# Two buffers for the triangular inversion, row lengths on GpSimd, state sums on TensorE and ScalarE

## The chip, the cores and the metric

The kernel runs on one NeuronCore of a Trainium2 chip. The core has a matrix engine (TensorE, "PE" in the profile, its weight loads "PEld"), a vector engine (VectorE, "DVE"), an activation engine (ScalarE, "ACT"), a general engine (GpSimd, "POOL") and an engine that here only issues transfers (SyncE, "SP"). Each engine takes its instructions strictly in the order of its own queue and waits at the head of that queue for what an instruction needs. Matrix products land in PSUM, which GpSimd can't read in this kernel; everything else lies in SBUF. The metric is the device time of one execution in microseconds (us); lower is better.

## The reference

A gated-delta recurrence over 32 sequences (4 batches of 8 heads, 768 steps, heads of 48), and then a router that sends each of 3072 tokens to two of eight experts:

```python
k_n = k / (np.linalg.norm(k, axis=-1, keepdims=True) + 1e-06)
for t in range(S):
    kt, vt, bt = (k_n[:, :, t], v[:, :, t], beta[:, :, t, None])
    y[:, :, t] = np.einsum('bhd,bhde->bhe', q[:, :, t], state)
    v_old = np.einsum('bhde,bhd->bhe', state, kt)
    state = state + bt[:, :, :, None] * np.einsum('bhd,bhe->bhde', kt, vt - v_old)
...
logits = x @ w_gate
noisy_logits = logits + np.log1p(np.exp(x @ w_noise)) * noise
top2 = np.argpartition(-noisy_logits, 2, axis=1)[:, :2]
...
h = np.maximum(x[mask] @ w1[e], 0.0)
out[mask] += top2_w[mask, k, None] * (h @ w2[e])
```

## The kernel before

**Two stages.** `deltanet` computes the recurrence, the router's choice, and the sending of each token's row to its experts' lists in memory. After it the experts run one after another: products on TensorE that fill it almost wholly. The change touches `deltanet` alone.

**How the recurrence is tiled.** The 768 steps are cut into 12 chunks of 64 (`c`). A unit `n` is one chunk for two of the four batches, so a chunk has two units (`z` 0 and 1). Two chunks, that is four units, make a block `s`; there are six blocks, 0 to 5. Within a chunk the recurrence is a triangular system, which the kernel inverts once for a whole block: 128 triangles of 32 by 32, one on each partition.

**What one block does.**
- `products` (from L509): the keys are transposed on TensorE, multiplied with themselves into a pair of PSUM banks, and ScalarE copies the diagonal squares to `gd` (L546).
- `begin_inversion` and `invert` (L559 to L661), on VectorE: a transposition of `gd` to `t` (L563); the diagonal of `t` is the squared lengths of the keys, copied to `ss` (L581, L582); ScalarE makes the root from logarithm and exponential (L585, L586); eight small VectorE operations make the length `norm`, `d` (beta over length squared) and `minus_d` (L591 to L602); GpSimd meanwhile zeroes all but the lower triangle of `t` (L610); `norm` is transposed to `norms` (L624); `t` is multiplied by `minus_d` (L629); then 30 columns, each a product into `part` (L641) and an addition to `t` (L645); the diagonal is set to one and `t` multiplied by `d` (L657).
- `end_inversion`: two transpositions of `t`, to `tb` (L667) and `tt` (L675).
- `join`: from `tb` and `tt`, TensorE and ScalarE put the 64 by 64 inverses `w64` together (L698 to L736).
- `within`: products of queries and keys, masked by VectorE to `qk` (L760).
- `recur`, once for each unit, the chain of the recurrence: GpSimd scales `v` by the lengths (L779); for `c > 0`, TensorE multiplies the old state by the keys (L517) and VectorE subtracts that from `v` (L798); TensorE solves with `w64` (L808); ScalarE copies the result `u` (L815); TensorE multiplies the keys by `u` into the pair of banks `p_s` (L826); VectorE adds the old state and writes the new one (L838, for the first chunk a copy, L842); GpSimd copies the state in a wider form to `wide` (L851).
- `answer`: the output rows `y`, their transposition and the router's logits.

`route` follows for blocks 0 and 1 together, 2 and 3 together, 4, and 5: some thirty small VectorE operations (L964 to L1041), and then GpSimd's indirect transfers that send the rows (L333, "spread" below; 16 for two blocks, 8 for one). `early` runs five tiles of expert 0 at the end of the stage, on rows that blocks 0 to 4 have sent (loads at L1178, first TensorE work L1206).

**Buffers.** `gd` has two buffers (`two_gds`), `t` has one (`t_inv`), and so have `ss`, `root`, `norm`, `d` and `minus_d`. So the transposition to `t` for a block stands behind `tb` and `tt` of the block before.

**What sets the order.** The pieces are not run as written: `Jobs.order` is a planner that places every piece on its engine with a cost and, for some, a due time, and the program then has each engine's queue in the order that it found. A block's transposition to `t` is due at `FIRST + s * PACE` (13 and 36 us). GpSimd's pieces are also linked in that order.

Of the kernel before, what the change touches and what calls it, by code (L numbers as in the profile page):

```python
# [18 lines left out]
Q = 32  # L19
# [10 lines left out]
INVERSIONS = [(s, 1) for s in range(6)]  # L30
# [152 lines left out]
def kernel(  # L183
# [84 lines left out]

    ones = const.tile([128, 128], FP32, name="ones")
# [110 lines left out]
    def deltanet(ictx):  # L380
# [68 lines left out]
        two_gds = ring([128, UH, Q], "gd", 2)  # L449
        most_steps = max(x for _, x in INVERSIONS)  # L450
        inversion_of = {s + x: g for g, (s, n) in enumerate(INVERSIONS) for x in range(n)}
        t_inv = sb([128, most_steps, Q, Q], "t")
        parts = sb([128, most_steps * 240], "part")
# [69 lines left out]
        def products(n):  # L523
# [14 lines left out]
            gd = two_gds(s).rearrange("p (u j z) i -> p u z j i", u=US, z=2)[:, i]  # L538
            for x, lo in enumerate(range(0, 128, Q)):
                rows, cols = slice(lo, lo + Q), slice(lo % C, lo % C + Q)  # L540
                on, copy = (DVE, nc.vector.tensor_copy) if s == 0 and x % 2 else (
                    ACT, nc.scalar.copy
                )
                jobs.add(
                    on, 0.38,
                    lambda rows=rows, cols=cols, copy=copy: copy(  # L546
                        gd[rows], two_banks(p, C)[rows, :, :, cols]
                    ),
                    writes=[("gd", s % 2, i, lo)], uses=p,
                )  # L550
# [5 lines left out]
        def begin_inversion(s):  # L556

            first_s, steps = INVERSIONS[inversion_of[s]]
            x = s - first_s  # L559
            gd = two_gds(s)  # L560
            jobs.add(
                DVE, 1.95,
                lambda: nc.vector.transpose(  # L563
                    out=t_inv[:, x], in_=gd.rearrange("p h i -> p i h")
                ),
                reads=[("gd", s % 2, i, lo) for i in range(US) for lo in range(0, 128, Q)],
                writes=["t"], due=FIRST + first_s * PACE + 2 * x,
            )

        def invert(g):  # L570

            first_s, steps = INVERSIONS[g]
            t, v_ = t_inv[:, 0:steps], nc.vector
            diagonal = t.rearrange("p s i j -> p s (i j)")[:, :, 0 : Q * Q : Q + 1]
            ss, root, norm, d, minus_d = (x[:, 0:steps] for x in small.values())
            shape = [128, steps, Q, Q]
            soon = FIRST + first_s * PACE + 2 * steps + 1.0
            per = 1.06 * steps

            def squares():  # L580
                v_.tensor_copy(ss, diagonal)  # L581
                v_.tensor_scalar_max(root, ss, 1e-30)  # L582

            def by_log():
                nc.scalar.activation(root, root, ACTF.Ln)  # L585
                nc.scalar.activation(root, root, ACTF.Exp, scale=0.5)  # L586

            def lengths():


                v_.reciprocal(norm, root)  # L591
                v_.tensor_tensor(out=norm, in0=norm, in1=ss, op=ALU.mult)
                v_.tensor_tensor(out=norm, in0=norm, in1=root, op=ALU.add)
                v_.tensor_scalar(
                    out=norm, in0=norm, scalar1=0.5, scalar2=1e-6, op0=ALU.mult, op1=ALU.add
                )
                v_.tensor_tensor(out=d, in0=norm, in1=norm, op=ALU.mult)
                v_.reciprocal(d, d)
                v_.tensor_tensor(
                    out=d, in0=d, in1=beta_b[:, first_s : first_s + steps], op=ALU.mult  # L600
                )
                v_.tensor_scalar_mul(minus_d, d, -1.0)  # L602

            jobs.add(DVE, 0.4, squares, reads=["t"], writes=["ss", "root"], due=soon)
            jobs.add(ACT, 0.5, by_log, writes=["root"], due=soon + 1)

            for x in range(steps):
                jobs.add(
                    POOL, 1.5,
                    lambda x=x: [nc.gpsimd.affine_select(  # L610
                        out=t[:, x], in_=t[:, x], pattern=[[1, Q], [-1, Q]], base=0,
                        channel_multiplier=0, compare_op=ALU.is_gt, fill=0.0,
                    )],
                    reads=["ss"], writes=["t"], due=soon + 3,
                )
            every_beta = [("beta", i) for i in range(128 // H)]
            jobs.add(
                DVE, 2.0, lengths, reads=["root", "ss", *every_beta], writes=["norm", "d"],
                due=soon + 3,
            )  # L620
            for x in range(steps):
                jobs.add(
                    DVE, 0.2,
                    lambda x=x: v_.transpose(out=norms(first_s + x), in_=norm[:, x]),  # L624
                    reads=["norm"], writes=[("norms", (first_s + x) % 3)],
                )
            jobs.add(
                DVE, 0.15 + per,
                lambda: v_.tensor_tensor(  # L629
                    out=t, in0=t, in1=minus_d[:, :, None, :].to_broadcast(shape), op=ALU.mult  # L630
                ),
                reads=["d"], writes=["t"],
# [3 lines left out]
            def column(j):  # L636
                shape = [128, steps, Q - 1 - j, j]
                part = parts[:, 0 : steps * shape[2] * j].rearrange(
                    "p (s i j) -> p s i j", s=steps, j=j
                )  # L640
                v_.tensor_tensor(  # L641
                    out=part, in0=t[:, :, j + 1 :, j, None].to_broadcast(shape),
                    in1=t[:, :, None, j, 0:j].to_broadcast(shape), op=ALU.mult,
                )
                v_.tensor_tensor(  # L645
                    out=t[:, :, j + 1 :, 0:j], in0=t[:, :, j + 1 :, 0:j], in1=part, op=ALU.add
                )

            for j in range(1, Q - 1):
                jobs.add(  # L650
                    DVE, 0.36 + 0.0019 * steps * j * (Q - 1 - j), lambda j=j: column(j),
                    writes=["t", *(("column", first_s + x, j) for x in range(steps))],
                )
            jobs.add(DVE, 0.2, lambda: v_.memset(diagonal, 1.0), writes=["t"])
            jobs.add(
                DVE, 0.15 + per,
                lambda: v_.tensor_tensor(  # L657
                    out=t, in0=t, in1=d[:, :, :, None].to_broadcast(shape), op=ALU.mult
                ),
                reads=["d"], writes=["t"],  # L660
            )  # L661

        def end_inversion(s):
            x = s - INVERSIONS[inversion_of[s]][0]
            jobs.add(
                DVE, 1.95,
                lambda: nc.vector.transpose(  # L667
                    out=tbs.rearrange("p h j -> p j h"),
                    in_=t_inv[:, x].rearrange("p i j -> p j i"),
                ),  # L670
                reads=["t"], writes=["tb"],
# [3 lines left out]
                lambda: nc.vector.transpose(  # L675
                    out=tts.rearrange("p h i -> p i h"), in_=t_inv[:, x]
                ),
                reads=["t"], writes=["tt"],
# [88 lines left out]
        def recur(n):  # L767
# [54 lines left out]
            def gather_state():  # L822
                for j in range(NP):
                    for y in range(2):
                        for b in range(2):
# [3 lines left out]
                                start=(j == 0), stop=(j == NP - 1), skip_group_check=True,  # L829
# [3 lines left out]
                PE, 0.55, gather_state, reads=[u_key, *halves("k", n % NK)], opens=p_s  # L833
            )

            def add_state():
                if c:
                    nc.vector.tensor_tensor(  # L838
                        out=new, in0=two_banks(p_s, D), in1=old, op=ALU.add
                    )  # L840
                else:
                    nc.vector.tensor_copy(new, two_banks(p_s, D))  # L842

            jobs.add(
                DVE, 0.58, add_state, reads=[("st", z, c % N_ST)] if c else [],
# [14 lines left out]
        def answer(n):  # L860
# [71 lines left out]
        small = {  # L932
            x: sb([128, most_steps, Q], x) for x in ("ss", "root", "norm", "d", "minus_d")
        }
# [388 lines left out]
        for s in range(NS):  # L1323
            units = range(s * US, (s + 1) * US)
            g = inversion_of[s]
            if s == INVERSIONS[g][0]:
                for x in range(s, s + INVERSIONS[g][1]):
                    for n in range(x * US, (x + 1) * US):
                        if x:
                            load(n, "k")  # L1330
                        products(n)
                    begin_inversion(x)
                invert(g)
                for x in range(s, s + INVERSIONS[g][1]):
                    for j, cost, moves, emit, writes in large.get(x, ()):
                        jobs.add(
                            SP, cost, emit, writes=writes, lands=2.0, moves=moves,
# [559 lines left out]
```

## Time and profile before

| what | value |
|---|---|
| runs | 870.63, 875.58, 874.54 us; median 874.54 us |
| the profiled execution | 876.77 us, of it 875.0 us span |
| mean granted TensorE clock over the span | 0.905 of full speed |
| busy over the span | TensorE 785.2, VectorE 499.5, ScalarE 309.8, GpSimd 311.4 us |
| start of the transposition to `t`, blocks 0 to 5 | 17.17, 52.01, 98.47, 139.05, 187.78, 230.64 us |
| start of the transposition to `tt`, blocks 0 to 5 | 50.06, 96.09, 136.68, 185.80, 228.62, 287.28 us |
| first TensorE work of `early` | 326.23 us |

The page of a profile gives each engine's busy time, then the span in 40 equal slices with one digit each for the busy share in tenths, and then groups of equal instructions with the number of them, their mean duration, and how long the engine stood idle just before them and who ended that. The table's starts are from the timeline of the trace. About the first 330 us are the recurrence, the rest the experts.

### The profile page before, as it was taken

How to read it: one execution, taken by the hardware profiler on the slowest of the kernel's cores; microseconds unless marked ns; L12 is line 12 of the kernel's file. 1: busy time of each engine (PE TensorE's matmuls, PEld its weight loads, DVE VectorE, ACT ScalarE, POOL GpSimd, SP SyncE). 2: the span in 40 equal slices, each digit the busy share in tenths (PEclk: the TensorE clock that was granted, in tenths of full speed). 3: DMA queues.
4: the chain of work that ended last, by engine and by line, in shares of the span. 5: the costliest groups of instructions: out<-in, count | busy, mean ns of one | idle time of the engine just before them, and what ended most of it. 6: DMA issues, size and time to landing. Idle time of an engine off the chain costs nothing. (4 is left out here: it accounts for less than half of the span.)

```text
span 875.0 us, 21652 instructions
## 1 busy us (share of the span) xinstructions
PE 785.2 (90%) x9166; PEld 602.0 (69%) x9166; DVE 499.5 (57%) x1153; ACT 309.8 (35%) x735; POOL 311.4 (36%) x328
## 2 busy tenths in 40 slices
PE   4758879886899898999999999999999999999995
PEld 3547768685788784566587587587587597597594
DVE  5987798979998632027554454454454454454441
ACT  3573558835743642111420420420420420410510
POOL 3021212021553735025425525525525525515311
PEclk8556759965789798999999999999999999999998
DMA  3789633724433223606324224224225223101201
GB/s 65 134 242 245 137 98 103 196 44 128 130 94 75 105 88 125 244 24 224 102 73 151 92 81 156 78 82 165 66 88 163 60 82 117 57 19 39 56 19 42
DMA packets 119085, 93.77 MB, mean 107 GB/s; under 512 B 84646, under 2 KB 109255, under 8 KB 118976
## 3 DMA queue, kind: packets, MB, share of 16 engines
q1 hardware_dynamic: 107312, 64.54, 26.8%
q0 software_dynamic: 9552, 27.33, 9.2%
q8 instruction: 74, 1.21, 0.6%
q10 hardware_dynamic: 2112, 0.39, 0.3%
q14 instruction: 35, 0.29, 0.1%
HBM read 58.82 MB, written 34.81 MB: 107 GB/s over the span
## 5 line engine op out<-in xcount | busy, mean ns | idle before, releaser
L374 POOL DMA_INDIRECT out_dram<-sums,index x49 | 48.5, 991 | 161.6 <-DVE sums L1386 138.8
L645 DVE TENSOR_TENSOR t<-t,part 128x30 f32<-128x30 f32 (+9 forms) x180 | 66.0, 367 | 6.2
L1498 PE MATMUL a<-xe,w1e 128*128 128x416 f32 x168 | 69.3, 521 | 0.0
L641 DVE TENSOR_TENSOR part<-t 128x30 f32<-128x30 f32 (+9 forms) x180 | 62.1, 345 | 5.0
L365 POOL DMA_INDIRECT sums<-out_dram,index x49 | 50.5, 1031 | 34.1 <-issue 24.0
L851 POOL COPY wide<-st 64x384 f32<-64x384 f32 x44 | 24.6, 559 | 105.3 <-DVE st L838 80.8
L333 POOL DMA_INDIRECT rows_x<-y,slot x48 | 47.1, 981 | 30.3 <-DVE early_gate L353 9.7
L1568 ACT COPY part_c<-c 128x416 f32<-128x416 f32 x28 | 14.2, 506 | 120.9 <-PE c L1498 120.9
L1498 PEld LDWEIGHTS a<-xe,w1e 128*128 128x128 f32 x168 | 29.6, 189 | 31.4 <-issue 17.8
L1559 DVE TENSOR_TENSOR hT<-part,d 128x416 f32<-128x416 f32 x28 | 16.3, 586 | 57.7 <-ACT part L1576 56.2
L1386 DVE SCALAR_TENSOR_TENSOR sums<-d,gate,sums 128x192 f32<-128x192 f32 x56 | 23.3, 416 | 42.5 <-PE d L1498 42.5
L1553 ACT ACTIVATE hT<-hT 128x416 f32<-128x416 f32 x84 | 45.1, 550 | 4.3 <-DVE hT L1559 1.8
L1535 ACT COPY xe<-x 128x384 f32<-128x384 f32 x21 | 10.1, 479 | 100.1 <-PE x L1530 100.1
L808 PE MATMUL single<-v,w 64*64 64x48 f32 x768 | 34.7, 253 | 9.6 <-ACT w L736 3.3
L1498 PE MATMUL d<-xe,w1e 128*128 128x416 f32 x112 | 41.6, 513 | 0.0
L1498 PE MATMUL c<-xe,s_w 128*128 128x416 f32 x112 | 41.4, 512 | 0.0
L1559 DVE TENSOR_TENSOR hT<-part,c 128x416 f32<-128x416 f32 x28 | 16.5, 588 | 41.8 <-ACT part L1587 40.2
L808 PEld LDWEIGHTS single<-v,w 64*64 64x64 f32 x768 | 32.2, 169 | 11.5 <-issue 5.5
L698 ACT COPY w<-tt 32x256 f32<-32x256 f32 x96 | 38.6, 402 | 1.7
L1498 PE MATMUL d<-t_w,hT 128*128 128x192 f32 x224 | 38.6, 326 | 0.0
L610 POOL TENSOR_SCALAR_AFFINE_SELECT t<-t 128x1024 f32<-128x1024 f32 x6 | 7.6, 1272 | 85.7 <-DVE ss L581 52.1
L1459 POOL TENSOR_TENSOR t_w<-w2e,t_w 128x768 f32<-128x768 f32 x14 | 25.4, 1815 | 32.4 <-PE x L1498 32.3
(241 smaller groups left out, 1884.2 us busy)
## 6 DMA issues: line engine op xcount, KB each, us to landing
w1e<-in_moe_w_dram SPq DMA_DIRECT2D x8, 1536.0 KB
w2e<-in_moe_w_dram SPq DMA_DIRECT2D x8, 1536.0 KB
xr<-rows_x SPq DMA_DIRECT2D x7, 1164.0 KB
rows_x<-empty SPq DMA_DIRECT2D x8, 776.0 KB
qp<-in_q_dram SPq DMA_DIRECT2D x48, 96.0 KB
v<-in_v_dram SPq DMA_DIRECT2D x48, 96.0 KB
out_dram<-empty SPq DMA_DIRECT2D x4, 1152.0 KB
kp<-in_k_dram SPq DMA_DIRECT2D x44, 96.0 KB
```

The costliest lines, as they stand in the source:

```text
L333: d = nc.gpsimd.indirect_dma_start(out=rows_x, out_offset=bass.IndirectOffsetOnAxis(ap=slot, axis=0), in_=rows, in_offset=None,).ins
L365: nc.gpsimd.indirect_dma_start(out=got, out_offset=None, in_=out, in_offset=bass.IndirectOffsetOnAxis(ap=index, axis=0), bounds_check=N - ...
L374: nc.gpsimd.indirect_dma_start(out=out, out_offset=bass.IndirectOffsetOnAxis(ap=index, axis=0), in_=got, in_offset=None, bounds_check=N - ...
L641: v_.tensor_tensor(out=part, in0=t[:, :, j + 1 :, j, None].to_broadcast(shape), in1=t[:, :, None, j, 0:j].to_broadcast(shape), op=ALU.mult,)
L645: v_.tensor_tensor(out=t[:, :, j + 1 :, 0:j], in0=t[:, :, j + 1 :, 0:j], in1=part, op=ALU.add)
L698: lambda rows=rows, cols=cols, w64=w64, tt=tt: nc.scalar.copy(w64[rows, :, cols], tt[rows]),
L808: nc.tensor.matmul(per_head(p_u)[b, h], w64[b, h], v_n[b, h], start=(h == 0), stop=(h == H - 1), skip_group_check=True,)
L851: nc.gpsimd.tensor_copy(wide[rows, :, :, y * D : (y + 1) * D], new[rows])
L1459: nc.gpsimd.tensor_tensor(out=out, in0=a, in1=b, op=ALU.subtract)
L1498: nc.tensor.matmul(p, lhsT, rhs, start=opens and i == 0, stop=i == len(products) - 1, skip_group_check=True,)
L1553: relu = lambda m, l, src: nc.scalar.activation(hT[:, m, half[l]], src, ACTF.Relu)
L1559: nc.vector.tensor_tensor(out=hT[:, m, half[l]], in0=x, in1=y, op=ALU.add)
```

## The change

**Inversion.** `gd` gets one buffer and `t` two, and the small tiles come in two sets. The transposition to `t` is due 6 us earlier (`EARLIER`). The lengths are made by one piece of twenty small operations on GpSimd, each on 128 partitions by 32 elements: a copy, six operations with constants and thirteen with two tensors, two of these a power (exponents -0.5 and -1, held in a tile `powers`). The power's root is refined by two Newton steps, the inverse by one. The triangle is cut (affine select) by GpSimd behind that piece in its queue. ScalarE's logarithm and exponential and VectorE's small operations of the inversion are gone.

**States.** For `c > 0` TensorE first multiplies the old state by the identity into the two banks, two products of 128 by 128 by 192, and the products of keys and `u` are added on top; ScalarE copies the sum to the new state. VectorE has no part in it.

**Order.** The planner is given the new costs, so the queues come out in another order. In the built kernel the transposition to `t` for block 1 stands on VectorE's queue behind column 12 of block 0, for block 2 right behind `tt` of block 0, for block 3 behind column 20 of block 2, for block 4 just ahead of `tb` and `tt` of block 3, and for block 5 behind column 24 of block 4.

```diff
-INVERSIONS = [(s, 1) for s in range(6)]
+EARLIER = 6.0
...
+    powers = const.tile([128, 2], FP32, name="powers")
+    for i in range(2):
+        nc.vector.memset(powers[:, i : i + 1], (-0.5, -1.0)[i])
...
-        two_gds = ring([128, UH, Q], "gd", 2)
-        t_inv = sb([128, most_steps, Q, Q], "t")
+        gds = sb([128, UH, Q], "gd")
+        t_invs = ring([128, Q, Q], "t", 2)
...
-            def squares():
-                v_.tensor_copy(ss, diagonal)
-                v_.tensor_scalar_max(root, ss, 1e-30)
-
-            def by_log():
-                nc.scalar.activation(root, root, ACTF.Ln)
-                nc.scalar.activation(root, root, ACTF.Exp, scale=0.5)
-
-            def lengths():
-                v_.reciprocal(norm, root)
-                v_.tensor_tensor(out=norm, in0=norm, in1=ss, op=ALU.mult)
-                v_.tensor_tensor(out=norm, in0=norm, in1=root, op=ALU.add)
-                v_.tensor_scalar(
-                    out=norm, in0=norm, scalar1=0.5, scalar2=1e-6, op0=ALU.mult, op1=ALU.add
-                )
-                v_.tensor_tensor(out=d, in0=norm, in1=norm, op=ALU.mult)
-                v_.reciprocal(d, d)
-                v_.tensor_tensor(
-                    out=d, in0=d, in1=beta_b[:, first_s : first_s + steps], op=ALU.mult
-                )
-                v_.tensor_scalar_mul(minus_d, d, -1.0)
...
+            soon = FIRST + s * PACE - EARLIER
+            def lengths():
...
+                made = [
+                    g.tensor_copy(ss, diagonal),
+                    ts(root, ss, 1e-30, 0.0, ALU.max),
+                    tt(root, root, power(0), ALU.pow),
+                ]
+                for _ in range(2):
+                    made += [
+                        tt(d, ss, root), tt(d, d, root), ts(d, d, -0.5, 1.5), tt(root, root, d),
+                    ]
+                return made + [
+                    tt(norm, ss, root), ts(norm, norm, 1.0, 1e-6),
+                    tt(root, norm, norm), tt(d, root, power(1), ALU.pow),
+                    tt(minus_d, root, d), ts(minus_d, minus_d, -1.0, 2.0), tt(d, d, minus_d),
+                    tt(d, d, beta_b[:, s]), ts(minus_d, d, -1.0, 0.0),
+                ]
...
+            jobs.add(
+                POOL, 3.4, lengths, reads=[*mine("t"), *every_beta],
+                writes=mine("norm", "d"), due=soon + 4,
+            )
+            jobs.add(
+                POOL, 1.5,
+                lambda: [nc.gpsimd.affine_select(
+                    out=t, in_=t, pattern=[[1, Q], [-1, Q]], base=0, channel_multiplier=0,
+                    compare_op=ALU.is_gt, fill=0.0,
+                )],
+                reads=mine("d"), writes=mine("t"), due=soon + 5,
+            )
...
             def gather_state():
+                if c:
+                    for b in range(2):
+                        nc.tensor.matmul(
+                            two_banks(p_s, D)[:, b], ident, old[:, b], start=True, stop=False,
+                            skip_group_check=True,
+                        )
                 for j in range(NP):
...
-                                start=(j == 0), stop=(j == NP - 1), skip_group_check=True,
+                                start=(j == 0 and not c), stop=(j == NP - 1), skip_group_check=True,
...
-            def add_state():
-                if c:
-                    nc.vector.tensor_tensor(
-                        out=new, in0=two_banks(p_s, D), in1=old, op=ALU.add
-                    )
-                else:
-                    nc.vector.tensor_copy(new, two_banks(p_s, D))
-
             jobs.add(
-                DVE, 0.58, add_state, reads=[("st", z, c % N_ST)] if c else [],
+                ACT, 0.5, lambda: nc.scalar.copy(new, two_banks(p_s, D)),
                 writes=[("st", z, (c + 1) % N_ST)], closes=p_s,
             )
```

## The prediction

> **What bounds the kernel now.** First the span in 40 slices (a digit is the busy share of a slice of 21.9 us in tenths):
>
> ```profile
> PE   4758879886899898999999999999999999999995
> DVE  5987798979998632027554454454454454454441
> PEclk8556759965789798999999999999999999999998
> ```
>
> VectorE is at 7 to 9 in the slices behind the first up to the thirteenth (285 us), TensorE at 9 from the seventeenth on, with the clock at 9. So two stages: up to about 290 us VectorE is mostly the fullest, behind it TensorE. What shortens the first moves the second forward and leaves it as long as it is. The windows, cut at the starts of the inversions, say the same with numbers (the columns are window, length, busy us and count for TensorE, weight loads, VectorE, ScalarE, GpSimd, then granted clock, transfer share, GB/s):
>
> ```profile
> 52.00:98.00 46.00, 33.80 (x967) 30.45 (x966) 37.43 (x88) 20.97 (x52) 9.01 (x13) 0.69 0.94 252
> 98.00:139.00 41.00, 33.40 (x873) 29.52 (x872) 34.75 (x87) 27.70 (x73) 6.75 (x9) 0.67 0.40 93
> 139.00:188.00 49.00, 43.50 (x1148) 38.77 (x1146) 43.21 (x116) 32.18 (x84) 8.56 (x13) 0.84 0.56 140
> 188.00:231.00 43.00, 32.64 (x810) 27.79 (x808) 35.96 (x90) 26.07 (x67) 11.27 (x16) 0.62 0.35 96
> 231.00:289.00 58.00, 51.91 (x1566) 47.06 (x1564) 52.59 (x133) 27.27 (x71) 30.77 (x40) 0.94 0.38 102
> 289.00:331.00 42.00, 36.25 (x953) 31.66 (x953) 18.77 (x72) 25.37 (x74) 23.52 (x28) 0.88 0.30 104
> ```
>
> TensorE is not far behind VectorE, at a clock that is often low; the reader should keep that for the rivals. Third, who VectorE waited for from 17 to 290 us, which is nearly all of its idle time that has a name:
>
> ```profile
> DVE norm L591 <- ACT root L586: 14.3, 6, 4.6
> DVE v L798 <- PE pair L517: 4.9, 4, 2.9
> DVE st L842 <- PE pair L826: 1.4, 1, 1.4
> ```
>
> 14.3 us are waits for ScalarE's root, 6.3 us for the recurrence.
>
> **What comes off VectorE.** The ten small operations of an inversion have mean rows of 188 (L581), 194, 353, 397, 286, 274, 420, 352, 191 and 181 ns (L602), together 2.84 us, six times 17.0 us. The wait for the root goes with them, 14.3 us. Of the state sums
>
> ```profile
> L838 DVE TENSOR_TENSOR st<-pair,st 128x384 f32<-128x384 f32 x20 | 10.7, 546 | 0.0
> ```
>
> 18 start before 289 us, 9.8 us, and the two copies of L842 1.1 us. Gross: 17.0 + 14.3 + 10.9 = 42.2 us.
>
> **What is paid for it, by parts.**
>
> *1. The first block has no cover.* Before, 3.4 us lie between the end of the transposition to `t` (19.1 us) and its multiplication (22.5 us), and they are in the gross. Now twenty GpSimd operations and the affine select stand there. No row has these shapes: copies of 128x8 to 128x16 on GpSimd took 0.17 to 0.20 us each where nothing held them, a product of 128x384 took 0.83 us. I take 0.2 us for eighteen. A power has no row; between a plain operation, 0.2 us, and GpSimd's longest elementwise row (t_w, 128x768, 1.8 us) I take 0.4 us, as it has 32 columns. So 18 x 0.2 + 2 x 0.4 = 4.4 us of lengths, with the affine select (1.27 us) and 0.3 us of signals 6.0 us (4.6 to 9.2).
>
> *2. The affine select runs beside columns.* At 235.78 us one stood beside a VectorE operation on two SBUF tensors:
>
> ```profile
> 235.67 1.29 POOL L610 TENSOR_SCALAR_AFFINE_SELECT t<-t 128x1024 f32<-128x1024 f32 x1
> 235.78 1.22 DVE L592 TENSOR_TENSOR norm<-norm,ss 128x32 f32<-128x32 f32 x1
> ```
>
> L592 takes 0.21 us alone, so it lost 1.0 us. Five blocks, one of which paid this before: 4 us (0 to 6.4).
>
> *3. The lengths run beside columns.* Columns are operations on two SBUF tensors too. What GpSimd's product does to one:
>
> ```profile
> 203.16 0.93 DVE L645 TENSOR_TENSOR t<-t,part 128x150 f32<-128x150 f32 x1
> 203.09 0.83 POOL L779 TENSOR_TENSOR v<-v,norms 128x384 f32<-128x384 f32 x1 [1.40 <-DMA v<-in_v_dram]
> ```
>
> L645 of this shape takes 0.32 us alone: 0.61 us lost in a GpSimd operation of 0.83 us. By columns that is 0.05 us for 32, and thirteen such operations with seven cheaper ones make 0.8 us for a block, 4 us for five (2 at the least, 22 if each of the 4.4 us falls on VectorE).
>
> The Trainium skill, in "SBUF — State Buffer", section "SBUF: two separate sides", speaks against the change here: VectorE operations with two SBUF inputs and GpSimd operations share a port pair under an exclusive lock, and the loser blocks for the whole instruction. By that rule all 4.4 us of a block fall on VectorE, 22 us, and the sum below would be 18 us worse, slower than before. The row at 203 us shows a block of three quarters of the instruction, so part of it runs outside of the lock; how much of a small one does, no row shows.
>
> *4. The recurrence of block 0 starts later.* `tt` of block 0 ends 2.6 us later by part 1 (6.0 less 3.4), 2.0 us by block 1's transposition among its columns, and 2 us by parts 2 and 3, so 6.6 us. The multiplication of block 1 comes at 52.0 + 6.6 + 2.0 (block 2's transposition), as before at 59.9. Behind it VectorE reaches the first subtraction from `v` (L798, 77.1 us before, 25 us behind `tt`) and there it already waited, 5 us with L842. It now waits about 5 us more (0 to 8): block 1's own saving is spent there.
>
> *5. Block 4's cover is short.* Between its transposition and its multiplication stand only `tb`, `tt` and some seven short operations, 3.9 + 1.4 us, against 4.4 + 1.3 us and whatever GpSimd loses to the lock: 1.5 us (0 to 5). Blocks 1, 2, 3 and 5 have 10 us and more of columns there.
>
> *6. The tail.* The choice of route for blocks 2 and 3 stood ahead of the last inversion's end: its slots were made at 280.6 us, with `tt` at 287.3 us. In the new queue they stand behind `tt`. So GpSimd's sixteen sends, 1.27 us apart, end some 8 us later against `tt`, and the first loads of `early` (318.9 us, which wait for the last send) with them. Half is covered by TensorE, busy 36.25 of 42 us in that window: 3.5 us (0 to 8). Queued behind these sends are `v` and `wide` of the last chunks; in the new queue four sends stand ahead of `v`, before there were nine, so the recurrence itself loses little.
>
> *7. TensorE.* Forty more products of 128x192, 326 ns each at full clock (row of the experts' L1498 at that shape), 13 us, at half clock up to 26 us. ScalarE gets 22 copies of 128x384 at 0.48 us and loses the logarithms, +8 us; its 46 to 68% use from 52 to 231 us covers that, and without cover it would cost 8 us. From 98 to 289 us TensorE is busy 161.5 of 191 us; after the savings there are about 167 us, and some 9 us are added. It fits only because the clock rises with density: 33 ns for each product at clock 0.94 (231 to 289 us), 40 ns at 0.62 (188 to 231 us). I charge 5 us (0 to 15).
>
> **Sum.** 42.2 - 6.0 - 4 - 4 - 5 - 1.5 - 3.5 - 5 = 13.2 us off the profiled execution's 876.8 us, 863.6 us. That execution lies 2.2 us above the median of the runs, so against the median 861.3 us; I say 862 us. With all parts at their low ends the gain is 36 us, at their high ends the change loses 31 us. Neither will happen in all parts together; from 5 to 28 us of gain, 847 to 870 us, is the likeliest case's own range.
>
> **The rivals.**
>
> *A, TensorE or the recurrence takes VectorE's place.* For it: 161.5 us of work in 191 us, the low clock, the later choice of route in the new queue, which says that the recurrence lags the inversions. Against: TensorE's time shrinks as it is filled. If it does not, and half of the former 29.5 us of idle time stays, the stretch can't be shorter than 161.5 + 9 + 15 = 185.5 us: 5.5 us gained, less the tail's 3.5: 872 us.
>
> *B, slower: GpSimd's small operations block the columns.* Place: the columns beside which the lengths run, in five blocks. Price: at 4.4 us whole, 22 us instead of 4, and the gain of 13 becomes a loss of 5. If the lock also holds GpSimd back behind each column, lengths take 8 us: 3.6 us more in block 0 and 3.6 in block 4. Together about 12 us slower, 887 us. It decides once VectorE loses over (13.2 + 4) / 5 = 3.4 us to the lengths of a block. A power of over 5 us each would do the same by parts 1 and 5. For it: the 1.0 us at 235.78 us. Against: `wide` copies of 0.6 us at 214.8 us cost two columns 0.2 us each.
>
> *C, everything is covered.* The recurrence of block 0 catches up by its shorter path (state sums no longer queue behind columns), the clock goes to full, the tail keeps its length: parts 4, 6 and 7 fall away, 13.5 us more gain: 848 us, and with the locks of part 3 at their low end 846 us.
>
> **How the numbers follow.** Likeliest case 0.56, A 0.17, B 0.18, C 0.09. A measurement here tells from no change what is over 0.5%, 4.4 us. The likeliest case and C are faster, and so are 0.07 of A; 0.10 of A and 0.01 of B lie within; 0.17 are slower. So 0.72, 0.11, 0.17. The range runs from C's 846 us to 880 us, which takes in B's price at 4.4 us of lengths.
>
> **What would show it.** The inversions' starts closer by 5 to 8 us from block 2 on, and hardly at block 1; the wait for L586 gone from VectorE and a wait of about 5 us more for L517 in block 1; twenty GpSimd operations in 4 to 6 us, columns beside them longer by about 1 us a block; TensorE's clock higher between 98 and 270 us; the experts' stage as long as it is. I am wrong if the columns' mean rises from 0.36 us by over 0.05 us (360 of them, 18 us), if VectorE waits for GpSimd in several blocks, or if TensorE is the engine that VectorE waits for.

## The result, and the profile after

| kernel | median | lowest to highest, runs | profiled execution, its span |
|---|---|---|---|
| before | 875.06 us | 870.63 to 879.21, 4 | 876.77, 875.0 us |
| changed | 903.59 us | 898.90 to 905.59, 4 | 905.59, 903.9 us |

The changed kernel takes 1.0319 times as long (95% interval 1.0251 to 1.0388): slower by 28.5 us, where 12.5 us faster was forecast. Experiments 1 to 4 ran on a chip on which the kernel before took 873.97 us, the eight runs of experiments 5 to 9 on two others, on which it took 908.57 and 905.63 us; a kernel is therefore compared by its ratio to the kernel before on the same chip.

The busy shares in 40 slices, now of 22.6 us:

```profile
PE   4446988795895989999999999999999999999995
DVE  4396886974949622204564355355444444354342
PEclk9855779876996969999999999999999999999998
```

VectorE, at 7 to 9 in most of these slices before, now falls to 3 and 4 between the nines: it stands still again and again. The windows, cut near the starts of the transposition to `tt` (window, length, busy us and count for TensorE, weight loads, VectorE, ScalarE, GpSimd, then granted clock, transfer share, GB/s):

```profile
67.00:109.00 42.00, 31.59 (x876) 28.08 (x876) 32.35 (x72) 19.32 (x47) 26.75 (x34) 0.59 1.01 255
109.00:146.00 37.00, 32.87 (x938) 29.05 (x936) 33.03 (x75) 28.56 (x75) 15.28 (x21) 0.86 0.32 73
146.00:198.00 52.00, 42.89 (x1073) 37.64 (x1072) 41.27 (x102) 31.57 (x82) 18.39 (x24) 0.82 0.49 132
198.00:254.00 56.00, 43.69 (x1221) 37.05 (x1220) 39.15 (x84) 31.61 (x79) 42.38 (x51) 0.83 0.48 131
254.00:308.00 54.00, 41.32 (x1085) 36.50 (x1086) 40.17 (x99) 24.13 (x63) 23.50 (x35) 0.84 0.19 43
```

In the last three windows VectorE is busy 120.6 of 162 us, and no other engine is fuller than TensorE's 127.9. So something waits. VectorE's waits from 17 to 320 us name it (us in total, times, longest):

```profile
DVE t L630 <- POOL t L618: 40.2, 4, 14.1
DVE norms L625 <- POOL norm L581: 9.6, 1, 9.6
DVE v L791 <- POOL v L772: 8.7, 2, 7.9
DVE v L791 <- POOL d L578: 6.3, 1, 6.3
```

The 14.3 us of waits for ScalarE's root are gone, and the waits for GpSimd are 64.8 us, where the kernel before had 7.2 us in the same window. L630 is the multiplication by `minus_d` (L629 before), L618 the triangle cut behind the lengths, L625 the transposition of `norm`, L772 the scaling of `v` and L791 the subtraction from it; L578 and L581 are the two helpers that issue the small operations. In GpSimd's timeline of block 0 (start, duration) one sees what takes so long:

```profile
18.82 0.23 POOL L589 COPY ss<-t 128x32 f32<-128x32 f32 x1 [10.68 <-DVE t L606]
...
19.58 5.46 POOL L578 TENSOR_TENSOR root<-root,powers 128x32 f32<-128x32 f32 x1
25.12 0.25 POOL L578 TENSOR_TENSOR d<-ss,root 128x32 f32<-128x32 f32 x1
...
28.68 5.42 POOL L578 TENSOR_TENSOR d<-root,powers 128x32 f32<-128x32 f32 x1
...
35.67 1.27 POOL L618 TENSOR_SCALAR_AFFINE_SELECT t<-t 128x1024 f32<-128x1024 f32 x1
```

Same line, same shape, 5.46 and 0.25 us: the two long ones are the powers. The other eighteen start about 0.33 us apart. The lengths take 16.9 us, and VectorE's multiplication starts at 36.98 us, against 22.53 before (first the line of before, then of the changed kernel):

```profile
22.53 1.22 DVE L629 TENSOR_TENSOR t<-t,minus_d 128x1024 f32<-128x1024 f32 x1
36.98 1.84 DVE L630 TENSOR_TENSOR t<-t,minus_d 128x1024 f32<-128x1024 f32 x1 [8.46 <-POOL t L618]
```

Where the span went is best read as a ledger of three times from the traces: the end of the last transposition to `tt`, the end of the last copy of `u` (the recurrence is done), and the span.

| kernel | last `tt` ends | last `u` ends (behind `tt`) | span (behind `u`) |
|---|---|---|---|
| before | 289.2 | 315.0 (25.8) | 875.0 (560.0) |
| changed | 308.1 | 349.9 (41.8) | 903.9 (554.0) |
| no powers (1) | 274.9 | 312.1 (37.2) | 866.1 (554.0) |
| state part alone (2) | 281.9 | 318.1 (36.2) | 878.2 (560.1) |
| state part taken back (3) | 305.6 | 333.6 (28.0) | 890.9 (557.3) |
| true cost in the plan (4) | 292.1 | 322.8 (30.7) | 881.8 (559.0) |

So of the 28.9 us more of span, 18.9 are lost by the inversions and 16.0 between the last inversion and the end of the recurrence, and 6.0 come back in the experts' stage.

### The profile page after: what moved, and what is told of

Same layout as the page of the kernel before. It is cut to its first block, busy times and chain, and to the rows that moved or that the text cites. A ratio compares the mean times of both kernels' runs of the same rounds, so it can differ in the third digit from the quotient of the medians.

```text
span 903.9 us, 21908 instructions
## 1 busy us (share of the span) xinstructions
PE 793.7 (88%) x9246; PEld 608.5 (67%) x9246; DVE 476.9 (53%) x1073; ACT 315.3 (35%) x745; POOL 408.9 (45%) x448
## 5 line engine op out<-in xcount | busy, mean ns | idle before, releaser
L644 DVE TENSOR_TENSOR t<-t,part 128x30 f32<-128x30 f32 (+9 forms) x180 | 68.7, 382 | 6.2
L640 DVE TENSOR_TENSOR part<-t 128x30 f32<-128x30 f32 (+9 forms) x180 | 66.9, 372 | 5.2
L548 ACT COPY gd<-pair 32x256 f32<-32x256 f32 x88 | 31.9, 362 | 26.6 <-PE pair L519 22.5
L519 PE MATMUL pair<-kT 64*64 64x64 f32 x768 | 22.6, 275 | 20.9 <-DVE qk L753 17.5
L711 PE MATMUL single<-tb,at 32*32 32x32 f32 x768 | 24.4, 219 | 16.6 <-ACT u L808 9.2
```

The costliest lines, as they stand in the source:

```text
L548: lambda rows=rows, cols=cols, copy=copy: copy(gd[rows], two_banks(p, C)[rows, :, :, cols]),
L640: v_.tensor_tensor(out=part, in0=t[:, j + 1 :, j, None].to_broadcast(shape), in1=t[:, None, j, 0:j].to_broadcast(shape), op=ALU.mult,)
L644: v_.tensor_tensor(out=t[:, j + 1 :, 0:j], in0=t[:, j + 1 :, 0:j], in1=part, op=ALU.add)
L711: nc.tensor.matmul(p_x()[dn, h], ats(n)[up, h % 2, h // 2], part_of(tbs, n)[up, h], start=(h == 0), stop=(h == H - 1), skip_group_check=True,)
```

## The experiments

Theory P: the powers. Rivals: S, the state part; C, GpSimd's small operations against VectorE's columns. Unless a number is called a ratio, times are medians.

**1. The powers left out.** Same queues, same number of operations.

```diff
-                    tt(root, root, power(0), ALU.pow),
+                    ts(root, root, -1.6, 2.4),
...
-                    tt(root, norm, norm), tt(d, root, power(1), ALU.pow),
+                    tt(d, root, root), tt(root, norm, norm),
```

> The changed kernel with the two powers of each block left out: the root starts from a straight line in the squared length (one operation with two constants) and the inverse from the square of the root, so the lengths keep twenty small operations in the same order and the queues do not change; the root is only good to some parts in a thousand. Theory P (the powers at 5.45 us each are what went wrong): a block's lengths take about 18 x 0.33 = 6 us in place of 17, block 0's first product (L630) starts near 26 us in place of 36.98, VectorE's wait for the triangle cut (L618, 40.2 us) falls below 10 us, and the time is 855 to 872 us. Theory S (state sums on TensorE and ScalarE, and the later recurrence, are the loss): that wait falls too, but the time stays at 885 us or more. Theory C (small GpSimd operations and VectorE's columns hinder each other): column means stay above 0.372 us and the time is 875 to 890 us.

Measured: 868.31 us against 873.97 (ratio 0.994, 0.9906 to 0.9973). The multiplication of block 0 starts at 26.07 us (first line). VectorE's waits in the same window as above follow, longest first:

```profile
26.07 1.23 DVE L630 TENSOR_TENSOR t<-t,minus_d 128x1024 f32<-128x1024 f32 x1 [2.96 <-POOL t L618]
...
DVE v L791 <- PE pair L519: 10.2, 3, 4.7
DVE v L791 <- POOL v L772: 8.0, 2, 7.2
DVE t L630 <- POOL t L618: 7.4, 3, 3.4
```

The wait for the triangle cut falls from 40.2 to 7.4 us, and the time by 35 us, more than the change had lost. P is shown; S asked for 885 us or more and falls as the main cause. The mean of the columns' additions and products is 391 and 387 ns, above C's mark of 372, but the time is below C's 875 us: the columns do pay, without deciding, and not to the lengths. In the trace of the changed kernel 55 column operations lie wholly within powers, and they took together 0.24 us longer than the quickest of their shapes; the 37 that touch a small operation of the lengths lost 0.53 us. They pay mostly to the scaling of `v`: the 15 columns that it overlaps more than any other GpSimd operation does lost 9.6 us, against 9 columns and 4.1 us before the change, and in this run 20 columns and 11.6 us.

**2. The state part alone**, put into the kernel before: the two products with the identity, ScalarE's copy, VectorE's additions gone.

> The kernel before with the state part alone: the old state goes to the PSUM pair by two products with the identity, ScalarE copies the sum. Theory P: this part is not the loss; VectorE sheds 10.9 us of additions, TensorE takes 40 products of 0.326 us more, and the time is 866 to 877 us against 875 before. Theory S: the longer step of the recurrence (two products and a copy behind it) shows at its full length 20 times, and the time is 882 us or more.

Measured: 880.01 against 873.97 us (1.0062, 1.0034 to 1.009): neither range was met. VectorE does get done earlier, the last `tt` ends 7.3 us sooner, but the recurrence ends 3.1 us later (36.2 us behind `tt` in place of 25.8). VectorE has been relieved of work that did not set the end.

**3. The state part taken back out of the changed kernel**, powers kept: the removed lines of the change's second half put back.

> The changed kernel with the state sums put back on VectorE (additions from PSUM, as before the change); powers and two buffers stay. Theory P: the time stays between 898 and 915 us, since the waits for GpSimd stay. Theory S: it falls to 890 us or less.

Measured: 892.96 us (1.0203, 1.0147 to 1.026), 10.6 us less than the changed kernel, between the two ranges. The waits for GpSimd stay (L618 17.0, L625 9.5, L772 22.3 us), so the powers stay the greater part, and the state part is a second loss: behind the last `tt` the recurrence needs 28.0 us, with the state part 41.8.

The traces show where. Before the change TensorE begins to join the last block (L718, now L711) 1.9 us behind `tt`; in the changed kernel, where `tt` ends at 308.1 us, its queue reads:

```profile
316.57 0.88 PE L865 MATMUL single<-wide,qT 128*64 128x96 f32 x16
319.69 1.94 PE L876 MATMUL single<-u,qk 64*64 64x48 f32 x32 [2.24 <-DVE qk L753]
...
327.04 1.16 PE L711 MATMUL single<-tb,at 32*32 32x32 f32 x34
```

The join stands ready for 18.9 us behind the outputs of block 4. These wait for VectorE's mask L753, that stands behind a subtraction, and the subtraction waits for GpSimd:

```profile
318.48 0.56 DVE L791 TENSOR_TENSOR v<-v,pair 128x384 f32<-128x384 f32 x1 [7.93 <-POOL v L772]
```

GpSimd in turn had stood at `wide` and a send before it came to `v` (three sends stand ahead of these lines):

```profile
315.80 0.50 POOL L843 COPY wide<-st 64x384 f32<-64x384 f32 x1 [2.57 <-DMA rows_x<-y,slot]
316.58 0.98 POOL L337 DMA_INDIRECT rows_x<-y,slot  x1 [0.28 <-POOL wide L843]
317.62 0.82 POOL L772 TENSOR_TENSOR v<-v,norms 128x384 f32<-128x384 f32 x1
```

The join starts behind `tt` by 1.9 us before, 18.9 us changed, 15.3 without powers (1) and 10.7 with the state part alone (2); in experiment 3, with the sums back on VectorE, it starts 3.6 us before `tt` has ended, as soon as `tb` is there. So on this chip the state part is dear in the order that the planner makes of it, at the end. Another order for the join was not tried.

**4. The planner told the truth.** The same instructions.

```diff
-EARLIER = 6.0
+EARLIER = 20.0
...
-                POOL, 3.4, lengths, reads=[*mine("t"), *every_beta],
+                POOL, 17.0, lengths, reads=[*mine("t"), *every_beta],
```

> The changed kernel where only the planner is told otherwise: the lengths cost 17.0 us in place of 3.4, and the transposition to t is due 20 us ahead in place of 6. The instructions are the same, in another order. Theory P with cover to be had: the powers are hidden from block 1 on, VectorE waits for the triangle cut (L618) in block 0 alone (about 14 us), and the time is 865 to 885 us. Theory P without cover (the transposition can't start early enough, or GpSimd's own queue is held up by the lengths): waits of 5 to 15 us stay in three or more blocks, or move to the scaling of v (L772) behind the lengths, and the time is 893 us or more.

Measured: 887.16 us (1.0151, 1.0104 to 1.0198), between the two ranges. The waits for the triangle cut are nearly gone, and a new one stands at the head:

```profile
DVE t L606 <- ACT gd L548: 16.8, 3, 15.1
DVE v L791 <- PE pair L519: 15.4, 4, 5.4
...
DVE t L630 <- POOL t L618: 2.9, 1, 2.9
```

The transposition that was to make the cover is now early for its own input, `gd`. A good half of the loss (903.6 to 887.2 of 28.5 us) came from an order made for lengths of 3.4 us and a transposition 6 us ahead; the two settings were not tried apart. The rest of the powers' price was not hidden so: block 0's multiplication still starts at 36.29 us.

**5. Both undone**: no powers, a third Newton step, and the state sums on VectorE by the edit of experiment 3 (not printed here).

```diff
-                    tt(root, root, power(0), ALU.pow),
+                    ts(root, root, -1.6, 2.4),
...
-                for _ in range(2):
+                for _ in range(3):
...
-                    tt(root, norm, norm), tt(d, root, power(1), ALU.pow),
+                    tt(d, root, root), tt(root, norm, norm),
```

> The changed kernel with both suspected parts undone: no powers (root from a straight line in the squared length, refined by three Newton steps, so 24 small operations and the root good to some parts in a million for these inputs; the inverse from the square of the root), and the state sums back on VectorE. Two losses that add: 868.3 us (no powers) less 6 to 10.6 us (what the state part cost alone, 880.0 - 874.0, and what taking it back gave, 903.6 - 893.0) plus 1 us for the third step: 858 to 864 us, and the stretch from the start of the last transposition to tt to the last copy of u falls from 39 us to about 28 us. If the state part costs only where VectorE has nothing else to wait for: 866 to 872 us.

Measured: 902.62 against 908.57 us (0.9936, 0.9895 to 0.9978). The 858 to 864 us would be ratios of 0.982 to 0.989: not met; the losses did not add. The other case, 866 to 872 us or 0.991 to 0.998, holds. Nor did the last stretch shrink to 28 us: the recurrence ended 36.6 us behind the last `tt`. Part of that belongs to the chip: on it, the kernel before with the seven operations of experiment 8 needs 34.7 us there, against 25.8 in the trace of the kernel before. In the traces from these two chips TensorE stood still for 12 to 18 us between 190 and 345 us ahead of products that waited for nothing that the profile names; in those of both kernels and of experiments 1 to 4 it was 1 to 7 us. Why was not found. It falls into the stretch that the change touches, so a small difference between ratios of different chips proves little. Repeated on the other of the two chips:

> The kernel without powers and with the state sums on VectorE once more. If 0.9936 holds: 0.989 to 0.998, and taking the state part out brings nothing beyond leaving the powers out (0.994). If two losses add: 0.981 to 0.988, as first expected.

Measured: 0.9951 (0.9917 to 0.9986), the same again: without powers this form gains half a per cent with the state part (experiment 1, on another chip) and without it.

**6. Lengths made as before the change** (VectorE and ScalarE), buffers and state part as changed.

> The changed kernel with the lengths made as before the change (ten small VectorE operations, logarithm and exponential on ScalarE); two buffers and the state part stay. If small VectorE operations lengthen the time one for one as the prediction has it (17.0 us over six blocks) and GpSimd's waits of the run without powers (7.4 + 4.5 us) go in return: 868.3 + 17 - 12 = 873 us, from 869 to 880 us. If the recurrence behind the last inversion sets the end and not VectorE: 864 to 869 us.

Measured: 911.86 against 908.57 us (1.0035, 0.9997 to 1.0073). 869 to 880 us would be 0.994 to 1.007, so the first case holds. Against experiment 1 (0.994) the small operations cost 0.0095, some 8 us, when they stand on VectorE. That speaks for GpSimd as their place, without powers; it compares two chips, and the recurrence here ends 51.8 us behind the last `tt`, so it is not shown.

**7. Two buffers alone**, lengths and state sums as before.

> Lengths and state sums as before the change; only two buffers for t, two sets of small tiles, one gd and the transposition 6 us earlier stay. If two buffers hide VectorE's wait for ScalarE's root (14.3 us before the change): 860 to 868 us. If the ordering gives that back (a block's transposition placed among the columns of the block before, ending that block later): 870 to 878 us.

Measured: 0.9944 (0.9905 to 0.9983), half a per cent faster, about 5 of the 14.3 us; the ranges as ratios were 0.984 to 0.993 and 0.995 to 1.004, so it lies between them. Once more, on the other chip:

> Two buffers alone once more (lengths and state sums as before the change), beside the others on one chip. The run before gave 0.9944 (0.9905 to 0.9983). If that holds: 0.990 to 0.998. If the longer times of that chip made it: 0.998 or more.

Measured: 0.9915 (0.9874 to 0.9956), the case that 0.9944 holds. In this trace the columns take 135.5 us against 128.1 before the change, though no length is made on GpSimd here; the new order alone puts 14 columns beside the scaling of `v` (9 before) and three beside the triangle cut (none before).

**8. The power by itself.** Operations on spare tiles, results unused:

```diff
+    for w in (8, 16, 32, 64):
+        nc.gpsimd.tensor_tensor(
+            out=probe_out[:, 0:w], in0=probe[:, 0:w], in1=probe[:, 0:w], op=ALU.pow
+        )
...
+        out=probe_out[0:32, 0:32], in0=probe[0:32, 0:32], in1=probe[0:32, 0:32], op=ALU.pow
...
+        out=probe_out[:, 0:32], in0=probe[:, 0:32], in1=probe[:, 0:32], op=ALU.mult
```

> The kernel before with seven operations on spare tiles added on GpSimd at its start, whose results are not used: powers on 128 partitions by 8, 16, 32 and 64 elements, on 32 partitions by 32, and an addition and a product on 128 by 32. If the power's cost is by the element along the row: 1.4, 2.7, 5.45, 10.9 us, and 5.45 us on 32 partitions, beside 0.25 us for the addition and the product. If it is a fixed cost of calling a power: about 5 us for all five.

The timeline of GpSimd:

```profile
2.60 1.68 POOL L276 TENSOR_TENSOR probe_out<-probe 128x8 f32<-128x8 f32 x1
...
7.41 5.41 POOL L276 TENSOR_TENSOR probe_out<-probe 128x32 f32<-128x32 f32 x1
...
12.93 10.51 POOL L276 TENSOR_TENSOR probe_out<-probe 128x64 f32<-128x64 f32 x1
...
23.56 5.41 POOL L279 TENSOR_TENSOR probe_out<-probe 32x32 f32<-32x32 f32 x1
...
29.43 0.23 POOL L285 TENSOR_TENSOR probe_out<-probe 128x32 f32<-128x32 f32 x1
```

From 32 to 64 elements a row it grows by 5.10 us, 0.16 us for each element of the row, with about 0.4 us beside that (16 elements took 2.92 us); 32 partitions cost as much as 128. A product of the same shape takes 0.23 us. It is a price by the element, as the first case had it.

**9. Mended: the root on ScalarE, the rest on GpSimd.** ScalarE's logarithm and exponential make the inverse root, one Newton step refines it, and the triangle cut no longer stands behind the lengths.

```diff
+            def by_log():
+                nc.scalar.activation(root, root, ACTF.Ln)
+                nc.scalar.activation(root, root, ACTF.Exp, scale=-0.5)
...
+                    tt(d, ss, root), tt(d, d, root), ts(d, d, -0.5, 1.5), tt(root, root, d),
+                    tt(d, root, root), tt(d, d, beta_b[:, s]), ts(minus_d, d, -1.0, 0.0),
+                    tt(norm, ss, root), ts(norm, norm, 1.0, 1e-6),
```

> A mended form of the changed kernel: GpSimd copies the squared lengths, ScalarE makes the inverse root (logarithm, exponential), GpSimd refines it by one Newton step and makes the lengths and factors in nine operations (11 on GpSimd in all, by 0.33 us: 3.7 us), the triangle cut stands ahead of them; state part as in the change. Theory P: as good as the run without powers or better: ratio to before 0.98 to 0.995, block 0's first product (L629 or L630) at 23 to 25 us. If small operations on GpSimd are no good place even without powers, because VectorE still waits for each of them: ratio 0.995 to 1.01.

Measured: 899.45 against 905.63 us (0.9923, 0.9891 to 0.9954); block 0's multiplication at 22.8 us. And with the state sums on VectorE:

> The same with the state sums back on VectorE. If the state part is a loss of its own (it cost 6 us alone): ratio 0.006 or more below that of the run with it, 0.975 to 0.989. If it costs nothing once the powers are gone (the runs without powers gave 0.994 with it and 0.9936 without it, on two chips): within 0.004 of it. If it is a gain once VectorE is the bound again: 0.005 or more above it.

Measured: 895.59 us (0.9842, 0.9781 to 0.9903), 0.008 below the form with the state part, though the two intervals just overlap. This is the lowest ratio of all forms, with its whole interval below 1; that of two buffers alone on the same chip (0.9874 to 0.9956) overlaps it too. The pair also suggests that VectorE is no longer the bound: with the state part the last `tt` ends at 270.8 us and the last `u` 58.6 us later, without it `tt` ends at 295.6 and `u` 33.2 us later, so both finish their recurrence at 329 us. (In the first of them 32 products of keys and `u`, L824, took 10.5 us from 277.25 us on while seven sends went out on GpSimd; its other such groups take 0.7 to 1.1 us. It is one of the stretches without a named wait of experiment 5, and it weakens the comparison.)

## Why the prediction was wrong

It failed at **part 1**, in one term: "A power has no row; between a plain operation, 0.2 us, and GpSimd's longest elementwise row (t_w, 128x768, 1.8 us) I take 0.4 us". Measured: 5.45 us. The upper bound was a row of another operation, and it was taken for a bound because that row was larger, although the power costs 0.16 us for each element of the row (experiment 8). The same part's other eighteen operations cost 0.33 us each by their spacing, not 0.2. Block 0's multiplication therefore came 14.4 us later, where part 1 and its 3.4 us of credit gave 2.6; without the powers it came 3.5 us later.

**Part 5** named the mechanism and the place ("Blocks 1, 2, 3 and 5 have 10 us and more of columns there") and was mis-sized by the same term: a cover of 10 us was enough for 5.7 us of lengths and cut, and not for 18. The multiplications of blocks 3, 4 and 5 waited 6.5, 14.05 and 11.2 us, where 1.5 us was charged for block 4.

**The gross** was right. VectorE's busy time fell by 22.6 us; the small operations (17.0) and the state sums (10.9) make 27.9, less 7.5 us by which the columns grew (128.1 to 135.6 us), which leaves 20.4 us. The wait for the root went too, and another took its place.

**Parts 2 and 3**, 8 us together, gave the right sum: the columns grew by 7.5 us in the changed kernel and by 11.9 us without powers. The rule of the Trainium skill ("SBUF — State Buffer", "SBUF: two separate sides") would, by the estimate made from it, have put 22 us on VectorE for lengths of 4.4 us; in the trace the columns beside the lengths lost 0.24 + 0.53 us in all (experiment 1). The measurement decides: neither powers nor small operations held the columns for long. So the size of parts 2 and 3 was right by luck, and its cause was not. The columns grew beside the scaling of `v`, 9.6 us in place of 4.1, and beside sends and the triangle cut, 1.9 and 0.9 us in place of 0.1 and none. The prediction's own row at 203 us was such a scaling; its price was carried over to the small operations, which barely hold a column, while the new order put more columns beside `v` itself.

**Part 4** foresaw 5 us more of waiting for L517 (now L519). In the changed kernel VectorE waited 3.7 us for it, since other waits came first, and 10.2 us without powers, against 4.9 before. At the place that part 4 named, the first two subtractions, it was 7.0 us without powers against 3.6 before: right in kind once the powers are gone, and somewhat less than 5 us more.

**Part 6**, the tail, was charged 3.5 us (0 to 8). The recurrence ended 16.0 us later behind the last `tt`, without powers 11.4 us. The late choice of route was there, but the sentence "the recurrence itself loses little" is what failed: the join of the last block stood behind outputs of block 4, whose states now come by TensorE and ScalarE. Experiments 2 and 3 tie this to the state part on their chip (experiment 5, on another, found no gain from taking it out), and with it **rival A** came true in part: without powers (0.994, A's 872 us would be 0.997) the recurrence had taken VectorE's place.

**Part 7**: the clock did rise, from 0.76 to 0.85 between 98 and 270 us and to 0.89 without powers, and in the changed kernel VectorE waited little for TensorE (3.7 us).

The sum without the mis-priced term comes near: 862 us forecast, 868.31 measured without powers, 6 us more. In part that is luck. By the ledger the inversions gained 14.3 us, where the sum has 16.7 ahead of the tail; the tail lost 11.4 us, where 3.5 was charged; and 6.0 us that nothing in the sum forecast came back in the experts' stage. **Rival B** had the direction and, in a half sentence ("A power of over 5 us each would do the same by parts 1 and 5"), the cause, but it got its chance from the lock and not from the power. That the high ends of all parts together gave a loss of 31 us, near the 28.5 lost, is chance. The range ended at 880 us because one unpriced operation was spread over small bounds.

## What to carry to other kernels

An operation without a row is not bounded by larger operations of another kind: where the queue of everything else hangs behind it, its price has to be measured first, or the forecast has to carry a case in which it is twenty times a product. Work that is moved to a free engine is free only while its cover is longer than it is; compare the two lengths block by block, the first block above all, and give a planner the true ones. And relieving the fullest engine pays only until the next chain: here the recurrence ended 3 us later and 3 us earlier where the last inversion ended 7 and 14 us earlier.

## What the hardware showed unasked

- A power on GpSimd costs 0.16 us for each element of a row whatever the number of partitions (5.41 us for 32 partitions and for 128), over twenty times a product (0.23 us).
- Small operations of 128 by 32 that follow each other on GpSimd start 0.33 us apart although each takes 0.25 us (block 0 of the changed kernel; 0.39 and 0.41 us apart in blocks 1 and 2).
- A GpSimd product of 128 by 384 (0.83 us) lengthened one column beside it by 0.61 us (at 203.16 us before) and another by 0.69 us (at 218.14 us in the changed kernel), while the 55 columns inside powers of 5.45 us lost 0.24 us together.
- The experts' stage became 6.0 us shorter behind the recurrence (560.0 to 554.0 us) in the changed kernel and without powers, by 2.7 and 1.0 us in experiments 3 and 4, and not with the state part alone. The first 20 us of `early` ran at a granted clock of 1.00 in place of 0.83; by an estimate from these two numbers that is 20 x 0.17 = 3.4 us, and the rest stays open.
- Open too: that the state part cost 6 and 10.6 us in experiments 2 and 3, about 7 in the pair of experiment 9, and nothing between experiments 1 and 5, which ran on two chips.
